# Halving a gated mixer's DFT steps by parity of 16-row blocks: small TensorE tiles for steps 1, 3 and 4, a product over all partitions, and a new hand-written order

## The chip, the core and the metric

The kernel runs on one core of one Trainium2 chip. The metric is device time in microseconds (us); the median of three runs before the change is 245.09 us (244.05 to 245.45). Five engines work side by side: TensorE (PE, with its weight loads PEld), VectorE (DVE), ScalarE (ACT), GpSimd (POOL) and SyncE (SP), which here issues all DMAs. Matmuls read SBUF (the on-chip memory of 128 partitions) and write PSUM, from which DVE or ACT must copy results out.

## The reference, cut to what matters

Two branches work on a sequence of S = 2048 rows of D = 640 channels, and a gate mixes them.

```python
x = A_q
g = sigmoid((x * gate_w).sum(-1, keepdims=True))
# branch A: a long convolution per channel, by FFT of length 2S
k_shift = sum of 4 shifted copies of k, each times shift_k[:, j]
kv = k_shift * v
y  = irfft(rfft(kv, 2S) * rfft(ssm_k, 2S))[:S] + kv * ssm_D
a  = q * y
# branch B: an MLP with shifts of the hidden rows
h  = gelu(layernorm(x) @ w1);  hs = (4 groups of h shifted by +1, -1, +2, -2 rows) @ w2
x1 = x + hs;  b = x1 + gelu(layernorm(x1) @ w3) @ w4
out = g * a + (1 - g) * b
```

All inputs and the output are bf16.

## The kernel before, in words

**Rows.** Row s = 16 t + t1 lies in partition t (0 to 127) at place t1 (0 to 15) of the free dimension, so a tile of 128 partitions x 16 x 640 holds the sequence (`q_rows`, L62 to L65).

**Branch A, the convolution.** It is a DFT of length 4096 in two stages, a product, and the inverse in two stages.

- *Taps* (`tap`, L518): the four-tap shift as matmuls with diagonal weights; they use half the rows of the array each (64 x 128 tiles), one half per 64 channels. `k` comes in by `k_load` (L497), which transposes on PE (`transposed`, L553; "A": ACT copies out) or by DMA ("D").
- *Step 1* (`step1`, L357): the DFT over t. The weights F1 (L223) have one column set per parity of t; each set has zeros in the rows of the other parity, so every matmul uses the full 128 x 128 array (L369, 512 columns; L372, 256). It runs for kv ("KV") and for the filter ("HT0"), eight blocks c of two t1 each, five units a block. Each unit takes one PSUM bank and one copy to `stg` by ACT (L320) or DVE (L322); the block is sent to DRAM (S_x or S_h).
- The filter reaches step 1 through `h_transpose` (L332): 80 PE transposes of 128 x 128, copied out by ACT (L346).
- *Gather* (L387) reads S_x or S_h back with t1 among the partitions.
- *Step 2* (`step2`, L395): the twiddled DFT over t1, on tiles of 64 rows x 32 columns, eight side by side (L413). Real parts land in partitions 0 to 63, imaginary parts in 64 to 127.
- *Product* (L430): the complex product of filter and kv, five DVE instructions for each of eight s (L434 to L442); four of them work on 64 partitions x 2560 elements, since real and imaginary parts lie in different partitions.
- *Step 3* (L445): the first inverse stage, full 128 x 128 matmuls (L456) with the weights I, built by `table` (L304) from CMP; five units of 512 columns for each s, one PSUM bank each, copied to `gs` and sent to S_g.
- `gin` (L472) loads S_g; *step 4* (L803) is the last inverse stage: two accumulating full matmuls of 320 columns (L817; F4, L239, has zeros for the other parity), then scale, gate and multiply by q (L821 and L824 on ACT and DVE, or L827 on DVE), and a total into X (L831).

**Branch B.** `x_stats`, `x_norm`, `x_turn` (layer norm and transposes), `mlp1` (L641, matmul L651, gelu L654), `h_shift` (L695, copies on DVE; `turn`, L684, shifts across the row blocks), `w2` (L723: matmul L728, add L730, sum of squares L733), `x1_norm` (L735), `w3` (L770: L776, gelu L781), `w4` (L789: L794, add L796), `scale_x1` (L783), `store` (L786).

**PSUM.** Pool "psc" (L76) has four banks and serves taps, steps 1 to 4 and the transposes; pool "psm" (L77) has two tiles of two banks for mlp1, w2, w3 and w4. The SBUF ring "row" has four slots (L69) and serves kn, xn, stg, gs, q2 and the last part of gin.

**Order.** The string ORDER (L835) lists every piece of every step by hand, with the engine of each copy ("A" or "V") in the step's name; every engine gets its instructions in this order. SP's queue carries every DMA in the same order, so a DMA that waits for its data holds up all that stand behind it.

Of the kernel before, what the change touches and what calls it, by code (L numbers as in the profile page):

```python
# [16 lines left out]
P = 128  # L17
S = 2048
D = 640
# [22 lines left out]
def kernel(  # L42
# [19 lines left out]
    q_rows = A_q.rearrange("b (p t1) d -> (b p) t1 d", t1=NT)  # L62
    o_rows = out.rearrange("b (p t1) d -> (b p) t1 d", t1=NT)
    v_rows = A_v.rearrange("b (p t1) d -> (b p) t1 d", t1=NT)
    k_rows = A_k.rearrange("b (p t1) d -> (b p) (t1 d)", t1=NT)  # L65
# [19 lines left out]
    F1 = const.tile([P, 2, P], BF16, name="F1")  # L85
    F4 = const.tile([P, 2, H, 2], BF16, name="F4")
    CMP = const.tile([P, 2, NG, 2, 32], BF16, name="CMP")
# [55 lines left out]

    def load_h(dc):
        if "E" not in st:
            st["E"] = main.tile([P, DC * F], BF16, name="E", tag="W3")
        if dc < 3:
            st["HN", dc] = st["E"][:, dc * S:dc * S + S]
        else:
            hn = ring.tile([P, S], BF16, name="HN", tag="gt", bufs=GTB)  # L150
            st["HN", dc] = hn[:]
        SP.dma_start(out=st["HN", dc], in_=A_ssm_k[dc * P:(dc + 1) * P, :])

    def load_x(c):
        SP.dma_start(out=X[:, 4 * c:4 * c + 4, :], in_=q_rows[:, 4 * c:4 * c + 4, :])

    def load_x0(h):
        SP.dma_start(out=X[:, 2 * h:2 * h + 2, :], in_=q_rows[:, 2 * h:2 * h + 2, :])
# [64 lines left out]
    def f1_table():  # L223


        ts(col(24), bit(0), -1.0, 1.0)
        stt(col(29), bit(0), -1.0, pf[:])
        ts(pf2[:], col(29), 0.5)
        n = tab([P, H, 2], "n")
        ts(n[:, :, 0], R64[:, 0:H], col(29), pf2[:])  # L230
        ts(n[:, :, 1], n[:, :, 0], float(128 + 128), op0=ALU.add)
        ts(n[:, :, 0], n[:, :, 0], float(64 + 128), op0=ALU.add)
        f = ring.tile([P, P], BF16, name="f", tag="gt", bufs=GTB)
        yield from sin_table(f[:].rearrange("p (a b) -> p a b", b=2), n, 256)
        yield
        for r in range(2):
            ts(F1[:, r, :], f[:], bit(0) if r else col(24))

    def f4_table():  # L239
# [3 lines left out]
        stt(col(1), bit(2), 4.0, col(0))  # L243
        stt(col(1), col(1), -1.0, pf[:])
        ts(col(1), col(1), 0.25, 1.0)
        stt(col(1), bit(3), 2.0, col(1))
        stt(col(1), bit(4), -2.0, col(1))
        stt(col(1), col(0), 32.0, col(1))
# [3 lines left out]
        V.memset(F4[:], 0.0)  # L252
        yield from sin_table(F4[:, 0, :, 0], n, 256)
        A.activation(out=F4[:, 1, :, 1], in_=n[:], func=ACT.Sin, scale=TWO_PI / 256 * SH, bias=NPI[:])

    def t2_table():

        ts(col(8), bit(6), -1.0, 1.0)
# [8 lines left out]
        for c in range(2):  # L267
# [6 lines left out]
            yield from sin_table(CMP[:, 0, :, c, :], n, 8192)  # L274
            yield

    def i_tables():

        ts(col(12), bit(5), -1.0, 1.0)
        ts(col(18), bit(5), 4.0, 1.0)  # L280
        stt(col(18), LOW5, 256.0, col(18))
        for c in range(2):
            ts(col(20 + c), bit(6), 2048.0, 2048.0 * (1 - c) + 4096.0)
        ag = ring.tile([P, NG], F32, name="ag", tag="gt", bufs=GTB)
        ts(ag[:], R64[:, 0:NG], 4.0, col(18))
        odd = ag[:].rearrange("p (i j) -> p i j", j=2)[:, :, 1]
        ts(odd, odd, -2.0, op0=ALU.add)
        yield
        m = ring.tile([P, NG, 32], I32, name="m", tag="gt", bufs=GTB)
        V.tensor_tensor(out=m[:], in0=ag[:].unsqueeze(2).to_broadcast([P, NG, 32]),  # L290
                        in1=R64[:, 0:32].unsqueeze(1).to_broadcast([P, NG, 32]), op=ALU.mult)
        for c in range(2):
            n = tab([P, NG, 32], "n")
            ts(n[:], m[:], col(20 + c), op0=ALU.add)
            yield from sin_table(CMP[:, 1, :, c, :], n, 8192)
            yield
# [6 lines left out]

    def table(which, ev):  # L304

        st["I"] = pool("C").tile([P, NG, P], BF16, name="I")
        for o in range(2):
            o and (yield)
            scaled(ev[o], st["I"].rearrange("p g (j c k) -> p g j c k", j=2, c=2)[:, :, o], CMP[:, 1], bit(5) if o else col(12))
# [13 lines left out]

    def cuts(a, b):
# [7 lines left out]
    def h_transpose(dc):  # L332
        if "HT0" not in st:
            st["HT0"] = main.tile([P, NT * D], BF16, name="HT0", tag="RT")
        hv = st.pop(("HN", dc)).rearrange("p (t t1) -> p t1 t", t1=NT)
        dst = st["HT0"][:].rearrange("p (t d) -> p t d", t=NT)
        def make(hh):
            box = {}

            def first():  # L340
                ps = box["ps"] = psc.tile([P, 8, P], BF16, name="pst", tag="c")
                for i in range(8):
                    PE.transpose(out=ps[:, i, :], in_=hv[:, 8 * hh + i, :], identity=IDB[:])

            def second():
                A.copy(out=dst[:, 8 * hh:8 * hh + 8, dc * P:(dc + 1) * P], in_=box["ps"][:])  # L346
# [10 lines left out]
    def step1(name, c, ev):  # L357
# [3 lines left out]
        o = 2 * c * D  # L361

        def make(u):
            box = {}

            def first():
                ps = box["ps"] = psc.tile([P, 2, 256], F32, name="ps1", tag="c")
                if u < 4:
                    PE.matmul(ps[:].rearrange("p a b -> p (a b)"), lhsT=F1[:, u % 2, :], rhs=src[:, o + 512 * (u // 2):o + 512 * (u // 2) + 512], start=True, stop=True)  # L369
                else:  # L370
                    for r in range(2):
                        PE.matmul(ps[:, r, :], lhsT=F1[:, r, :], rhs=src[:, o + 1024:o + 1280], start=True, stop=True)  # L372

            def second():
                if not stg:
                    stg.append(ring.tile([P, 2, 2 * D], BF16, name="stg", tag="row", bufs=ROW))
                if u < 4:
                    evac(ev[u], stg[0][:, u % 2, 512 * (u // 2):512 * (u // 2) + 512], box["ps"][:].rearrange("p a b -> p (a b)"))
                else:
                    evac(ev[u], stg[0][:, :, 1024:1280], box["ps"][:])  # L380
            return first, second

        def send():
            SP.dma_start(out=scr[:, :, o:o + 2 * D], in_=stg[0][:])
        return banks(5, make, [send])
# [9 lines left out]
    def step2(name, b, ev):  # L395
# [5 lines left out]
        def make(u):  # L401
            ps = []

            def first():
                for j in range(2):
                    ps.append(psc.tile([P, 512], F32, name="ps2", tag="c"))
                for lo, hi in cuts(512 * u, 512 * u + 512):
                    i = lo // D
                    for o in range(2):
                        for c in range(2):  # L410
                            for j in range(2):
                                q, r = H * c + 32 * o, slice(H * j, H * j + H)
                                PE.matmul(ps[j][q:q + 32, lo - 512 * u:hi - 512 * u], lhsT=CMP[r, 0, 8 * b + 2 * i + o, c, :],  # L413
                                          rhs=ax[i // 2][r, 2 * (i % 2) + o, lo - i * D:hi - i * D], start=True, stop=True, tile_position=(H * j, q))
# [15 lines left out]
    def product(s):  # L430

        h, x = st.pop(("hs", s)), st.pop(("xs", s))
        p2 = ring.tile([P, 4, D], BF16, name="p2", tag="HM", bufs=1)
        V.tensor_tensor(out=p2[0:64], in0=x[0:64], in1=h[64:128], op=ALU.mult)  # L434
        yield
        V.tensor_tensor(out=p2[64:128], in0=x[64:128], in1=h[0:64], op=ALU.mult)  # L436
# [3 lines left out]
        V.tensor_tensor(out=h[0:64], in0=h[0:64], in1=h[64:128], op=ALU.subtract)  # L440
        yield
        V.tensor_tensor(out=h[64:128], in0=p2[0:64], in1=p2[64:128], op=ALU.add)  # L442
        st["p", s] = h

    def step3(s, ev):  # L445
        p1 = st.pop(("p", s))
        gs = []

        def make(u):
            box = {}  # L450

            def first():
                ps = box["ps"] = psc.tile([P, 512], F32, name="ps3", tag="c")
                for a, b in cuts(512 * u, 512 * u + 512):
                    i = a // D
                    PE.matmul(ps[:, a - 512 * u:b - 512 * u], lhsT=st["I"][:, 8 * (s // 2) + 2 * i + s % 2, :], rhs=p1[:, i, a - i * D:b - i * D], start=True, stop=True)  # L456

            def second():
                if not gs:
                    gs.append(ring.tile([P, 4, D], BF16, name="gs", tag="row", bufs=ROW))  # L460
                evac(ev[u], gs[0][:].rearrange("p g d -> p (g d)")[:, 512 * u:512 * u + 512], box["ps"][:])
            return first, second
# [5 lines left out]
        return banks(5, make, [send])  # L468
# [28 lines left out]
    def k_load(c, how):  # L497
# [4 lines left out]
        if how == "D":  # L502
            return [lambda: SP.dma_start_transpose(out=dst(), in_=k_rows[:, 4 * c * D:4 * c * D + 4 * D])]

        def load():
            st["kn", c] = ring.tile([P, 4 * D], BF16, name="kn", tag="row", bufs=ROW)
            SP.dma_start(out=st["kn", c][:], in_=k_rows[:, 4 * c * D:4 * c * D + 4 * D])
# [7 lines left out]
    def v_load(c):  # L515
        SP.dma_start(out=st["KV"][:, 4 * c * D:4 * c * D + 4 * D].rearrange("p (t d) -> p t d", d=D), in_=v_rows[:, 4 * c:4 * c + 4, :])

    def tap(q, ev):  # L518
# [17 lines left out]
        for e in range(2):  # L536
# [12 lines left out]
            steps += [copied, times] if ev[e] == "A" else [both]  # L549
# [3 lines left out]
    def transposed(dst, src, how):  # L553

        def make(u):
# [8 lines left out]
            def second():  # L564
                evac(how, dst()[:, a:b, :], box["ps"][:, 0:b - a, :])
# [118 lines left out]
    def turn(E, dst, src, s):  # L684

        if s > 0:
            E.memset(dst[:, :, 0:1], 0.0)
            E.tensor_copy(out=dst[:, :, 1:P], in_=src[:, :, 0:P - 1])
        else:
            E.memset(dst[:, :, P - 1:P], 0.0)  # L690
            E.tensor_copy(out=dst[:, :, 0:P - 1], in_=src[:, :, 1:P])
# [94 lines left out]
    def store(t1):  # L786
        SP.dma_start(out=o_rows[:, t1, :], in_=X1[:, t1, :])
# [10 lines left out]
    def load_q(c):  # L798
        q2 = ring.tile([P, 4, D], BF16, name="q2", tag="row", bufs=ROW)
        SP.dma_start(out=q2[:], in_=q_rows[:, 4 * c:4 * c + 4, :])  # L800
# [235 lines left out]
```

## Time and profile before

| What | Value |
|---|---|
| median of three runs | 245.09 us |
| profiled execution, span (its own time, from first to last instruction) | 240.0 us |
| first matmul starts | 6.58 us |
| last matmul ends | 235.9 us |
| step 1, 96 matmuls (L369, L372) | 16.1 + 3.5 us from start to start |
| step 2, 512 matmuls (L413) | 12.5 us from start to start |
| step 3, 64 matmuls (L456) | 10.0 us from start to start |
| step 4, 64 matmuls (L817) | 9.4 us from start to start |
| product, 40 instructions (L434 to L442) | 59.5 us busy on DVE |
| granted TensorE clock | 1.000 |

All durations in the profile are those of one execution, whose span is 5.1 us below the median of the runs. A matmul's busy time overlaps that of the next one, so PE's busy times of groups add up to more than the span; "from start to start" is the distance from the first matmul of an unbroken run of one line to the first of the next run, added over the runs. A group's row names the line, the engine, the operation, what is written and read, the shape, and the number; then the total busy time and the mean of one in ns; then how long the engine stood idle before.

### The profile page before, as it was taken

The page shows a single profiled execution, that of the slowest core. Times are in us where ns is not written, and L with a number is a line of the kernel's source. Part 1 is how long each engine was busy: PE and PEld are TensorE (multiplying, and loading weights), DVE is VectorE, ACT ScalarE, POOL GpSimd, SP SyncE. Part 2 cuts the span into 40 slices and gives each one's busy share as a digit, 9 for nine tenths or more (in the row PEclk, how much of TensorE's full clock was granted, in tenths as well). Part 3 has the DMA queues.
Part 4 walks back from the last instruction along what each step waited for, and adds up shares of the span by engine and source line. Part 5 has one row for each costly group of instructions (what it writes and reads, how often), then busy time and mean ns, then how long its engine had stood idle before and what let it go on. Part 6 is the DMA issues. An engine that isn't in the chain of part 4 may idle for free.

```text
span 240.0 us, 5176 instructions
## 1 busy us (share of the span) xinstructions
PE 224.6 (94%) x2041; PEld 122.6 (51%) x2041; DVE 209.6 (87%) x428; ACT 176.0 (73%) x300; POOL 11.1 (5%) x26
## 2 busy tenths in 40 slices
PE   0989999999999999999999999999999999999993
PEld 0975556444865555434444444455434456456551
DVE  7999999877889999769999999999999996247895
ACT  4999999779899999999949866837568642336430
POOL 1022012000000020004200000000000000000000
PEclk9999999999999999999999999999999999999999
DMA  7999999885879959995999836976410376489933
GB/s 248 392 373 221 371 324 268 203 288 202 242 224 379 405 199 225 317 335 171 294 271 248 247 130 232 200 264 223 145 54 0 128 231 219 137 297 279 304 110 109
DMA packets 48390, 57.05 MB, mean 238 GB/s; under 512 B 23017, under 2 KB 40170, under 8 KB 48110
## 3 DMA queue, kind: packets, MB, share of 16 engines
q1 hardware_dynamic: 48366, 56.72, 76.8%
q8 instruction: 16, 0.26, 0.4%
q14 instruction: 8, 0.07, 0.1%
HBM read 33.77 MB, written 18.36 MB: 217 GB/s over the span
## 4 chain that ended last, share of the span: by engine, by line
PE 40%; DVE 32%; ACT 18%; DMA 4%; issue 4%; SPq 0%; DVEq 0%
PE ps L776 13%; PE ps L794 8%; PE psm L651 7%; ACT stg L320 4%; DVE p L436 4%; DVE p L434 4%; ACT HT L346 3%; PE ps L369 3%; DVE X L796 3%; DVE hs L442 3%; DVE hs L440 3%; DVE hs L438 3%; ACT KT L320 3%; ACT jk L733 3%; DMA q<-in_A_q_dram 2%
## 5 line engine op out<-in xcount | busy, mean ns | idle before, releaser
L794 PE MATMUL ps<-W,gt 128*128 128x512 bf16 (+1 forms) x384 | 56.9, 299 | 0.0
L776 PE MATMUL ps<-x1t,W 128*128 128x512 bf16 x240 | 55.3, 379 | 0.7 <-DVE X L796 0.7
L794 PEld LDWEIGHTS <-gt 128*128 128x128 bf16 x384 | 29.6, 98 | 24.1 <-issue 2.8
L781 ACT ACTIVATE gt<-ps 128x1024 bf16<-128x1024 f32 x24 | 24.8, 1034 | 20.5 <-PE ps L776 20.5
L776 PEld LDWEIGHTS <-W 128*128 128x128 bf16 x240 | 22.5, 98 | 27.5 <-issue 3.4
L320 ACT CAST stg<-ps 128x512 bf16<-128x512 f32 x45 | 25.1, 637 | 0.7 <-PE ps L369 0.7
L322 DVE CAST stg<-ps 128x512 bf16<-128x512 f32 x35 | 22.8, 685 | 3.1 <-PE ps L369 2.9
L320 ACT CAST gs<-ps 128x512 bf16<-128x512 f32 x33 | 17.4, 598 | 11.0 <-PE ps L456 10.0
L651 PE MATMUL psm<-xt,WA 128*128 128x512 bf16 x100 | 23.5, 379 | 0.0
L728 PE MATMUL psw<-WA,HT 128*128 128x512 bf16 (+1 forms) x116 | 21.4, 299 | 0.0
L320 ACT CAST hs<-ps 128x512 bf16<-128x512 f32 x31 | 16.5, 615 | 2.5 <-PE ps L413 2.4
L322 DVE CAST XS<-ps 128x512 bf16<-128x512 f32 x21 | 13.4, 683 | 3.4 <-PE ps L413 3.3
L821 ACT ACTIVATE y<-ps,GS 128x320 bf16<-128x320 f32 x17 | 8.1, 526 | 10.9 <-PE ps L817 7.2
L827 DVE SCALAR_TENSOR_TENSOR q<-ps,GS,q 128x320 bf16<-128x320 f32 x15 | 7.8, 545 | 9.0 <-PE ps L817 8.2
L651 PEld LDWEIGHTS <-WA 128*128 128x128 bf16 x100 | 9.6, 97 | 11.2 <-issue 0.6
L728 PEld LDWEIGHTS <-HT 128*128 128x128 bf16 x116 | 10.0, 98 | 10.0 <-issue 0.7
L796 DVE SCALAR_TENSOR_TENSOR X<-ps,OMG,X 128x640 bf16<-128x640 f32 x16 | 14.0, 878 | 0.2
L730 DVE SCALAR_TENSOR_TENSOR X<-psw,X 128x640 bf16<-128x640 f32 x16 | 12.9, 820 | 1.0 <-PE psw L728 1.0
L413 PE MATMUL ps<-ax,CMP 64*32 64x512 bf16 (+3 forms) x512 | 13.4, 300 | 0.1
L733 ACT ACTIVATE jk<-X 128x640 bf16<-128x640 bf16 x16 | 13.4, 834 | 0.0
L320 ACT CAST XS<-ps 128x512 bf16<-128x512 f32 x19 | 10.5, 606 | 3.1 <-PE ps L413 3.1
L654 ACT ACTIVATE HT<-psm 128x1024 bf16<-128x1024 f32 (+1 forms) x12 | 10.5, 885 | 3.0 <-PE psm L651 3.0
(142 smaller groups left out, 377.7 us busy)
## 6 DMA issues: line engine op xcount, KB each, us to landing
S_x<-stg SPq DMA_DIRECT2D x8, 640.0 KB, 3.8
ax<-S_x SPq DMA_DIRECT2D x8, 640.0 KB, 5.2
S_h<-stg SPq DMA_DIRECT2D x8, 640.0 KB, 8.0
ax<-S_h SPq DMA_DIRECT2D x8, 640.0 KB, 4.4
S_g<-gs SPq DMA_DIRECT2D x8, 640.0 KB, 3.2
W<-in_B_w_dram SPq DMA_DIRECT2D x2, 1920.0 KB
KV<-in_A_v_dram SPq DMA_DIRECT2D x4, 640.0 KB
q<-in_A_q_dram SPq DMA_DIRECT2D x4, 640.0 KB
```

What stands on the lines that cost most here:

```text
L320: A.copy(out=dst, in_=src)
L322: V.tensor_copy(out=dst, in_=src)
L413: PE.matmul(ps[j][q:q + 32, lo - 512 * u:hi - 512 * u], lhsT=CMP[r, 0, 8 * b + 2 * i + o, c, :], rhs=ax[i // 2][r, 2 * (i % 2) + o, lo - i ...
L651: PE.matmul(ps[:, v, :].rearrange("p (a b) -> p a b", a=4), lhsT=W1N[:, k, 160 * f:160 * f + P] if f < 4 else W1M[:, k, :], rhs=xt[:, :, k ...
L654: A.activation(out=st["HT"][:, 4 * c:4 * c + 4, 2 * u:2 * u + nf, :].rearrange("p t f b -> p f t b"), in_=ps[:].rearrange("p f (t b) -> p ...
L728: PE.matmul(ps[:, o:o + w], lhsT=h_tile(f, t1), rhs=W2P[:, f, o:o + w], start=(f == 0), stop=(f == 4))
L730: V.scalar_tensor_tensor(out=X1[:, t1, :], in0=ps[:], scalar=1.0, in1=X[:, t1, :], op0=ALU.mult, op1=ALU.add, accum_out=S12[:, 0, t1:t1 + 1])
L733: A.activation(out=jk[:], in_=X1[:, t1, :], func=ACT.Square, accum_out=S12[:, 1, t1:t1 + 1])
L776: PE.matmul(ps[:, u, :].rearrange("p (a b) -> p a b", a=4), lhsT=st["W3"][:, k, f * P:(f + 1) * P], rhs=xt[:, :, k, :], start=(k == 0), st ...
L781: A.activation(out=gt[:, 2 * (fp % 2):2 * (fp % 2) + 2, :], in_=ps[:], func=ACT.Gelu_apprx_tanh)
L794: PE.matmul(ps[:, o:o + w], lhsT=st["gt", c, f // 4][:, f % 4, i * P:(i + 1) * P], rhs=st["W4"][:, f, o:o + w], start=(f == 0), stop=(f == ...
L796: V.scalar_tensor_tensor(out=X1[:, t1, :], in0=ps[:], scalar=OMG[:, t1:t1 + 1], in1=X1[:, t1, :], op0=ALU.mult, op1=ALU.add)
```

## The change

Rows are dealt differently: with s = 32 t2 + 16 r + t1, row s now lies in partition 64 r + t2 at place t1. So the parity r of the 16-row block is the half of the partitions. The parts:

- `both` (new): every load of q, k and v is issued as two DMAs of 64 partitions; `store` also. `load_cj`, weights and scratch transfers stay as they are.
- `turn` (shifts): a shift across row blocks is now two copies, since the neighbour in partition order is in the other half.
- `h_transpose`: 160 transposes with 64 weight columns, each into half of the PSUM partitions; the copies are spread over ACT and DVE.
- `step1`: F1 has 64 rows used for each parity; for every unit two matmuls of 512 columns, one on rows 0 to 63 and one on rows 64 to 127, each into a PSUM bank of its own. Four blocks of four t1 instead of eight of two.
- `step2`: the same 512 matmuls on the same tiles, but the output is ordered so that real and imaginary parts (c) stand in separate slots of the free dimension, over all 128 partitions.
- `product`: four of its five instructions are 128 partitions x 1280.
- `step3`: the weights INV (32 rows used per tile, made directly by `i_tables`; `table` and I are gone); two units for each s, each of 16 matmuls of 320 columns on tiles of 32 rows x 64 columns, which take four PSUM banks at once and are copied out in four pieces of 320.
- `step4`: two matmuls of 320 columns, each into half of the PSUM partitions, without zeros and without accumulation.
- `tap` and `step4` get an empty step for "V", so that the numbering of steps doesn't depend on the engine.
- ORDER is new throughout, engine letters too.

```diff
+    def both(dst, rows, t, n, at):
+        for r in range(2):
+            SP.dma_start(out=dst[HALF[r], at * D:(at + n) * D], in_=rows[r][:, t * D:(t + n) * D])
...
-                    PE.transpose(out=ps[:, i, :], in_=hv[:, 8 * hh + i, :], identity=IDB[:])
+                    for r in range(2):
+                        PE.transpose(out=ps[HALF[r], i, :], in_=hv[:, 8 * hh + i, r, :], identity=IDB[:], tile_position=(0, H * r))
...
-                if u < 4:
-                    PE.matmul(ps[:].rearrange("p a b -> p (a b)"), lhsT=F1[:, u % 2, :], rhs=src[:, o + 512 * (u // 2):o + 512 * (u // 2) + 512], start=True, stop=True)
-                else:
-                    for r in range(2):
-                        PE.matmul(ps[:, r, :], lhsT=F1[:, r, :], rhs=src[:, o + 1024:o + 1280], start=True, stop=True)
+                for r in range(2):
+                    ps.append(psc.tile([P, 512], F32, name="ps1", tag="c"))
+                    PE.matmul(ps[r][:], lhsT=F1[HALF[r]].rearrange("p a b -> p (a b)"), rhs=src[HALF[r], o + 512 * u:o + 512 * u + 512], start=True, stop=True,
+                              tile_position=(H * r, 0))
...
-        V.tensor_tensor(out=p2[0:64], in0=x[0:64], in1=h[64:128], op=ALU.mult)
+        V.tensor_tensor(out=p2[:, 0, :], in0=x[:, 0, :], in1=h[:, 1, :], op=ALU.mult)
...
-        V.tensor_tensor(out=h[0:64], in0=h[0:64], in1=h[64:128], op=ALU.subtract)
+        V.tensor_tensor(out=h[:, 0, :], in0=h[:, 0, :], in1=h[:, 1, :], op=ALU.subtract)
...
-                ps = box["ps"] = psc.tile([P, 512], F32, name="ps3", tag="c")
-                for a, b in cuts(512 * u, 512 * u + 512):
-                    i = a // D
-                    PE.matmul(ps[:, a - 512 * u:b - 512 * u], lhsT=st["I"][:, 8 * (s // 2) + 2 * i + s % 2, :], rhs=p1[:, i, a - i * D:b - i * D], start=True, stop=True)
+                for i in range(4):
+                    ps.append(psc.tile([P, W], F32, name="ps3", tag="c"))
+                for c in range(2):
+                    for h in range(2):
+                        for i in range(4):
+                            a = slice(32 * i, 32 * i + 32)
+                            PE.matmul(ps[i][HALF[h]], lhsT=INV[a, 4 * (s // 2) + 2 * h + s % 2, 1 - c:3 - c, :].rearrange("p a b -> p (a b)"),
+                                      rhs=y[a, c, h, W * v:W * v + W], start=(c == 0), stop=(c == 1), tile_position=(32 * i, H * h))
...
-            E.tensor_copy(out=dst[:, :, 1:P], in_=src[:, :, 0:P - 1])
+            E.tensor_copy(out=dst[:, :, H:P], in_=src[:, :, 0:H])
+            E.tensor_copy(out=dst[:, :, 1:H], in_=src[:, :, H:P - 1])
...
-                    PE.matmul(ps[:], lhsT=F4[:, r].rearrange("p a b -> p (a b)"), rhs=g[:, r, o + 320 * v:o + 320 * v + 320], start=(r == 0), stop=(r == 1))
+                    PE.matmul(ps[HALF[r]], lhsT=F4[:], rhs=g[:, r, o + 320 * v:o + 320 * v + 320], start=True, stop=True, tile_position=(0, H * r))
```

In the new ORDER the five loads of the filter (`load_h`) stand together behind the second block of kv's step 1, where before they were spread over the first part; W4's load stands behind all of the filter's step-1 stores, where before two of these came after it; the last step of the list is now step 4's total of t1 = 12, where before it was the store behind w4's add of t1 = 15.

## Prediction

> **What bounds the kernel now.** I read the shares of each engine first, then the 40 slices, then windows of 15 us, then TensorE's own timeline.
>
> ```profile
> PE 224.6 (94%) x2041; PEld 122.6 (51%) x2041; DVE 209.6 (87%) x428; ACT 176.0 (73%) x300; POOL 11.1 (5%) x26
> ...
> PE   0989999999999999999999999999999999999993
> ...
> DVE  7999999877889999769999999999999996247895
> ACT  4999999779899999999949866837568642336430
> ```
>
> PE is full from the second slice to the last but one. VectorE is full too, up to slice 33, ScalarE mostly up to slice 22. The windows (stretch, its length, then busy us and instruction count of PE, PEld, DVE, ACT, POOL, then granted clock, DMA share, GB/s) show that PE stays full whichever of the others does. The chain of waits puts only 40% on PE because it goes through VectorE wherever both are full:
>
> ```profile
> PE 40%; DVE 32%; ACT 18%; DMA 4%; issue 4%; SPq 0%; DVEq 0%
> ```
> ```profile
> 120.00:135.00 15.00, 15.00 (x180) 6.94 (x178) 14.67 (x16) 11.85 (x20) 0.00 (x0) 1.00 1.07 271
> ...
> 195.00:210.00 15.00, 15.00 (x101) 8.10 (x99) 8.43 (x9) 3.61 (x5) 0.00 (x0) 1.00 0.62 197
> ```
>
> A busy PE can be a waiting PE, so I took distances from the start of one run of matmuls to the start of the next (first column below; the second column counts overlap).
>
> ```profile
> 46.20 2.32 PE L651 MATMUL psm<-xt,WA 128*128 128x512 bf16 x10
> 48.35 1.03 PE L369 MATMUL ps<-KV,F 128*128 128x512 bf16 x4
> 49.22 2.32 PE L651 MATMUL psm<-xt,WA 128*128 128x512 bf16 x10
> ```
> ```profile
> 97.34 2.32 PE L776 MATMUL ps<-x1t,W 128*128 128x512 bf16 x10
> 99.59 0.63 PE L413 MATMUL ps<-ax,CMP 64*32 64x512 bf16 x24
> 100.15 2.33 PE L776 MATMUL ps<-x1t,W 128*128 128x512 bf16 x10
> 102.41 0.85 PE L413 MATMUL ps<-ax,CMP 64*32 64x384 bf16 x32
> 103.19 2.33 PE L776 MATMUL ps<-x1t,W 128*128 128x512 bf16 x10
> 105.45 0.63 PE L413 MATMUL ps<-ax,CMP 64*32 64x512 bf16 x16
> ```
>
> Ten 512-column matmuls take 2.15 us between others of the full array (46.20 to 48.35): 0.2155 each. That is the price of 512 columns. Adding columns at this price over the whole kernel, with 0.117 us for each change of tile shape (worked out below), gives 216.3 us: transposes 10.6, taps 8.6, mlp1 21.6, z 1.1, step 1 17.3, w2 21.7, w3 51.7, step 2 8.6, step 3 8.6, step 4 8.6, w4 51.7, 52 changes 6.1. From the first matmul (6.58) to the end of the last (235.9) pass 229.3 us. So all waits inside PE's list are 13.0 us, 3.3 of them in the first 60 transposes (6.8 us for 3.5 of work, behind ScalarE's copies of KT). **PE's own list is the bound.** 240.0 is 6.6 of start, 216.3 of PE, 13.0 of waits and 4.1 of tail.
>
> **The price of a change of tile shape.** Step 2 is the one step in small tiles between full ones. Before it, ten w3 matmuls take 2.25 to 2.26 (97.34 to 99.59, 100.15 to 102.41) in place of 2.155: 0.10 more. Its own runs of 16 and 24 matmuls are two units of 512 columns with eight tiles side by side, 0.431 us, and take 0.56: 0.13 more. One excursion costs 0.233, one change 0.117. The taps (64 rows by 128 columns, L534) agree: 44 at 33.47 take 1.87 to 35.34, 1.72 of columns if both halves run side by side and 3.45 if not. So half-row tiles do run in pairs, and 0.14 goes to the change.
>
> **Part by part.**
>
> Step 1 (L369, L372; new L363). 64 matmuls of 512 and 32 of 256 columns, half of whose weight rows are zero, become 80 of 512 on half-row tiles: 40 pairs of 0.2155 = 8.6 in place of 17.3, **−8.7**. The taps are the row for the pairing; nothing side by side would be 0.
>
> Step 3 (L456; new L450). 64 full matmuls, 20,480 columns, 8.6 us, become 256 of 320 columns on eight tiles: 10,240 columns, 4.3 us, **−4.3**. The nearest row is step 2, 512 of 320 on average at 24 ns.
>
> Step 4 (L817; new L815). 64 of 320 columns, 8.6 us, now in pairs on half-column tiles: **−4.3**. Row: z_rows, 20 of 512 columns in 1.18 us, four side by side (4.3 one after another).
>
> The transposes of the filter (L343) go from 80 to 160 with 64 weight columns, in pairs: 5.0 again; one after another 160 × 62 ns = 10. I take 0, up to +5.
>
> Changes of shape. In the changed program's instruction order on PE I count them: 52 before, 159 after, because the step-1, step-3 and step-4 runs stand between full-array runs (25, 16 and 8 runs). 107 × 0.117 = **+12.5**. Below: 0, if they hide. Above: a single tap (19.87 to 21.09, 1.21 for 0.86) would make it 0.175 each, +18.7. I take the step-2 row, the only one with twenty repeats. PE's list: −8.7 −4.3 −4.3 +12.5 = **−4.8**, to 211.5.
>
> [...]
>
> VectorE. Product: five instructions of 1,488 ns (L434 to L442, four of them 64 partitions × 2560) become four of 128 × 1280 and one as before. Between 640 elements (L831, 483 ns) and 2560 (L438, 1,489) 1280 is 818: 8 × (7.44 − 4.76) = −21.4. Copies of step 3: 7 of 512 (687 ns) become 23 of 320, at most 545 each (L827): +7.7. Step-1 copies 35 to 25: −6.9. Seven copies of the filter's transposes come from ScalarE: +4.7 at the 676 of a 1024-wide xt copy (L322). Five x_norm (439) and three scale (382) more: +3.3; step 4: 8 fewer of 545, 8 more of 318: −1.8; tables about −4, the shifts' doubled copies +1. Two KT copies come too (+1.4), two of hs (+1.4). Together about −15. It buys nothing directly: PE was full in 120 to 135 while DVE was. ScalarE: ten copies of step 1 more (+6.4), seven HT copies fewer (−7.4), step-3 copies 33 × 598 to 41 × at most 526 (+1.9), step 4 +8 × 527 (+4.2), x_norm and scale −7.5, tables −3, but seven loads of function tables for four (3 × 1.28 = +3.9), KT and hs −3: about −4.5. Both have more slack; of the 9.7 us of waits inside the list after the first transposes I give back 2. Bounds: 0, and all 9.7.
>
> Start. Four issues of X stand before the first k in place of two (0.44 us each): kn may land 0 to 0.9 later. VectorE now takes two of nine KT copies, 1.8 us of ScalarE's 6.9. Together **−1.0** (between +0.9 and −1.8).
>
> Queue. SP issues 34 more DMAs (halves of 64 partitions): 34 × 0.45 = 15 us of its time. SP waits in line for its data nearly all the time, so this is hidden in the middle. In the tail 32 stores for 16 are about 13 us of issue in some 24. What stands behind them is load_q.3 and the last stores. The kernel now ends with a total (L829, 0.48) and two issues after w4's last add: **+0.9** (0 to 2).
>
> Moved loads. W4 was issued at 96.6, landed at 104.9 and was first read at 114.5; from the last step-1 run to the first w4 PE's list had 17.2 us and now has 14.0, so 9.6 of cover become about 6. The five loads of the filter (512 KB each), spread over 8.9 to 44 us before, now stand together some 10 us of PE's list ahead of their transposes; 2.5 MB at the 250 GB/s of slices 8 to 10 are 10 us. I take 0 for both; +3 if the filter is late, which the upper end below contains.
>
> **Sum.** 240.0 − 4.8 − 2.0 − 1.0 + 0.9 = 233.1 of span. The runs' median, 245.09, is 5.1 above the profiled span; with it **238.2 us**.
>
> **Rivals.**
> (a) Forecast: changes cost what step 2 shows, PE stays full: 235 to 242.5. Chance 0.44.
> (b) Changes cost less where only rows or only columns are cut, or the waits go as well: half of the 12.5 is −6, all of the waits −7.7 more: 225 to 234, middle 232. For it: DVE and ACT have slack. Against: the taps, rows only, pay 0.14 + 0.10. Chance 0.18.
> (c) PSUM slots become the bound, slower than before. The pool "psc" has four banks. Before, step 3 took one at a time (L453), now four at once; step 1 takes two. A step-3 run can't start until four copies are out, and the next unit of any step waits for its four. 14 of 16 runs have at least one copy on VectorE, behind a product instruction (1.49 or 0.82) or w4's add (0.88). It decides when the copies come out later than the w3 or w4 run between (1.6 to 2.2 us). At one short product instruction each, 14 × 0.8 = 11: 249. At one long one and an add, 14 × 2.4 = 33. Against: before, PE waited for step-3 copies only once, 0.3 us. Chance 0.25.
> (d) The tiles don't run side by side, the change doesn't do what it says: +17.3 and +5: 260. The taps and z speak against. Chance 0.05.
> (e) Halved DMAs eat it: the first 15 us and the tail are paced by SP, +6: 244. Chance 0.08.
>
> **Numbers.** Likeliest (a): 238.2, its own range 235 to 242.5. To leave out no more than 2 in 10 I go from 231 (within b) to 249 (within c). 0.5% is 1.2 us, about what a measurement of this kernel can tell. Faster by more: a and b, 0.62. Within: e, 0.08. Slower: c and d, 0.30.
>
> **What would show it.** Step-1 runs of four matmuls: 0.43 + 0.23 = 0.66 from start to start (0.86 if unpaired, 0.43 if changes are free). Step-3 runs of 16: 0.27 + 0.23 = 0.50. w3 runs of ten beside them 2.26. Product instructions of 1280 at 0.82. PE's span from first matmul to last about 222. Wrong if PE has waits over 0.5 us ahead of L450 or L363 released by gs or stg copies (c), or if step-3 runs take over 0.6 without a wait.

## The result and the profile after

The changed kernel takes 258.04 us (median; 257.56 to 258.53), the kernel before 244.57 in the same comparison: a ratio of 1.058, with a 95% interval of 1.052 to 1.065. The forecast was 238.2, range 231 to 249. The profiled execution of the kernel after has a span of 256.2 us.

Page of the kernel after: busy us of each engine, then the slices (PEclk is the granted TensorE clock), then the chain of waits by engine.

```profile
PE 223.2 (87%) x2278; PEld 114.3 (45%) x2297; DVE 193.4 (76%) x454; ACT 172.5 (67%) x310; POOL 13.0 (5%) x26
...
PE   0387789999899998999999999999999999579960
...
DVE  7757499889766878987789895888987974057970
ACT  0979399779966898899679776764674544145630
...
PEclk9999999999999999999999999999999999959995
...
PE 66%; DMA 17%; DVE 5%; ACT 5%; SPq 3%; issue 2%; DVEq 0%; ACTq 0%
```

VectorE lost 16.2 us of work and ScalarE 3.5, as forecast (15 and 4.5). PE was to stay full; it isn't in the first six slices, in the 35th and 36th and at the end. DMA rose from 4% to 17% of the chain, DVE fell from 32% to 5%.

To place the difference I cut the span at four events, read from PE's timeline: the first matmul, the filter's first transpose, the end of the last step-1 run, the start of w3's last 40 matmuls.

| Stretch, us | before | after | difference |
|---|---|---|---|
| start to first matmul | 6.58 | 9.60 | +3.0 |
| to the filter's first transpose | 54.3 | 59.2 | +4.8 |
| to the end of step 1 | 36.44 | 40.70 | +4.3 |
| to w3's last 40 matmuls | 106.86 | 102.93 | −3.9 |
| to the end of the last matmul | 31.67 | 34.99 | +3.3 |
| tail | 4.11 | 8.79 | +4.7 |

Of the rows that were to get shorter only the fourth did, and more than half of that is work that moved. One w3 run of ten matmuls stands ahead of the last step-1 run in the kernel after; before, all of w3 stood behind it (the timeline at 97.34 in the prediction).

```profile
106.65 2.33 PE L773 MATMUL ps<-x1t,W 128*128 128x512 bf16 x10
108.92 0.60 PE L363 MATMUL ps<-HT,F 64*128 64x512 bf16 x4
```

Its 2.27 us belong to the third row in one kernel and to the fourth in the other. With the same work in each row they would read +2.0 and −1.7. (The profiled execution of the kernel before was a quick one. The two kernels of the last experiments that start with the same DMAs have their first matmul at 8.15 and 8.16, so some 1.6 of the first +3.0 is spread. A span lies 1.8 below its own execution's time in the kernels run since, so a typical span of the kernel before is about 242.)

The end first. Windows of the kernel after (columns as in the prediction: PE, PEld, DVE, ACT, POOL, granted clock, DMA share, GB/s), and then its PE timeline:

```profile
221.20:225.60 4.40, 0.00 (x0) 0.00 (x0) 0.00 (x0) 0.00 (x0) 0.00 (x0) 0.73 0.97 307
225.60:230.00 4.40, 4.03 (x19) 2.01 (x21) 3.30 (x9) 2.81 (x5) 0.00 (x0) 0.50 1.02 405
```
```profile
213.69 7.50 PE L773 MATMUL ps<-x1t,W 128*128 128x512 bf16 x34
225.64 2.13 PE L815 MATMUL ps<-gin,F 128*64 128x320 bf16 x14 [4.45 <-DMA gin<-S_g]
228.11 3.52 PE L792 MATMUL ps<-W,gt 128*128 128x512 bf16 x11 [0.33 <-issue]
231.56 0.73 PE L815 MATMUL ps<-gin,F 128*64 128x320 bf16 x8
```

All engines stand still for 4.4 us while the DMAs are full: step 4 waits for gin. Behind it the granted clock is 0.50, and w4's first run takes 3.45 from start to start in place of 2.69. In the tail SP's timeline shows the last 24 half stores back to back:

```profile
237.48 16.17 SPq L785 DMA_DIRECT2D out_dram<-X  x24
```

That is 0.67 us each, to 253.65, while the last matmul ended at 247.4.

Now the start. One window each, from 7 to 15 us, of the kernel before and of the kernel after:

```profile
7.00:15.00 8.00, 7.26 (x88) 6.77 (x88) 7.67 (x21) 7.75 (x12) 1.22 (x2) 1.00 1.03 397
```
```profile
7.00:15.00 8.00, 4.61 (x40) 4.11 (x40) 5.32 (x13) 6.88 (x12) 2.85 (x2) 1.00 1.05 213
```

The last two columns decide. The DMA engines are as busy (1.03, 1.05), but they move 213 GB/s in place of 397. Busy DMA engines aren't fast ones here: the packets got slower (those of 5,120 bytes from a mean of 205 ns to about 370 in the first 15 us).

**Theory:** a DMA over 64 neighbouring partitions moves its bytes at half the rate, and that costs most of the loss; the rest is the unpaired transposes and the place of load_q in SP's queue. **Rivals:** the doubled distance of the rows in DRAM; SP's issues; a loss inside PE's list (the changes of tile shape, PSUM slots).

### The profile page after: what moved, and what is told of

Same layout as the page of the kernel before. It is cut to its first block, busy times and chain, and to the rows that moved or that the text cites. A ratio compares the mean times of both kernels' runs of the same rounds, so it can differ in the third digit from the quotient of the medians.

```text
span 256.2 us, 5750 instructions
## 1 busy us (share of the span) xinstructions
PE 223.2 (87%) x2278; PEld 114.3 (45%) x2297; DVE 193.4 (76%) x454; ACT 172.5 (67%) x310; POOL 13.0 (5%) x26
## 4 chain that ended last, share of the span: by engine, by line
PE 66%; DMA 17%; DVE 5%; ACT 5%; SPq 3%; issue 2%; DVEq 0%; ACTq 0%
PE ps L792 21%; PE ps L773 18%; PE psw L725 6%; DMA KV<-in_A_v_dram 5%; PE ps L403 5%; PE pst L337 4%; DMA X<-in_A_q_dram 4%; DMA S_h<-stg 3%; PE psm L646 3%; PE ps L363 3%; PE ps L450 3%; PE ps L815 3%; DMA S_g<-gs 2%; DMA gin<-S_g 2%; SPq L150 2%
## 5 line engine op out<-in xcount | busy, mean ns | idle before, releaser
L792 PE MATMUL ps<-W,gt 128*128 128x128 bf16 (+1 forms) x371 | 56.6, 300 | 1.4 <-issue 1.0
L310 ACT CAST stg<-ps 128x512 bf16<-128x512 f32 x55 | 29.7, 592 | 5.4 <-PE ps L363 4.7
L310 ACT CAST gs<-ps 128x320 bf16<-128x320 f32 x41 | 15.1, 433 | 15.5 <-PE ps L450 12.1
L725 PE MATMUL psw<-WA,HT 128*128 128x128 bf16 (+1 forms) x110 | 20.9, 296 | 1.3 <-DVE X L727 0.9
L819 ACT ACTIVATE y<-ps,GS 128x320 bf16<-128x320 f32 x25 | 11.8, 528 | 13.9 <-PE ps L815 13.2
L312 DVE CAST stg<-ps 128x512 bf16<-128x512 f32 x25 | 16.6, 683 | 3.0 <-PE ps L363 2.3
L312 DVE CAST gs<-ps 128x320 bf16<-128x320 f32 x23 | 10.5, 485 | 8.8 <-PE ps L450 7.7
L557 PE MATMUL pst<-IDB,kn 128*128 128x128 bf16 x60 | 7.0, 311 | 11.0 <-DMA kn<-in_A_k_dram 10.3
L725 PEld LDWEIGHTS <-HT 128*128 128x128 bf16 x116 | 9.3, 98 | 11.6 <-issue 4.1
L825 DVE SCALAR_TENSOR_TENSOR q<-ps,GS,q 128x320 bf16<-128x320 f32 x7 | 3.7, 548 | 13.4 <-PE ps L815 13.4
L529 PE MATMUL psk<-DG,KT 64*128 64x256 bf16 (+3 forms) x190 | 11.3, 244 | 2.5 <-ACT yk L537 1.7
```

Source lines behind the costliest of these rows:

```text
L310: A.copy(out=dst, in_=src)
L312: V.tensor_copy(out=dst, in_=src)
L529: PE.matmul(ps[e][:, lo:hi, :], lhsT=kt[a], rhs=st["DG"][a, 4 * k + lo - i:4 * k + hi - i, a], start=(i == 0), stop=(i == 7))
L725: PE.matmul(ps[:, o:o + w], lhsT=h_tile(f, t1), rhs=W2P[:, f, o:o + w], start=(f == 0), stop=(f == 4))
L792: PE.matmul(ps[:, o:o + w], lhsT=st["gt", c, f // 4][:, f % 4, i * P:(i + 1) * P], rhs=st["W4"][:, f, o:o + w], start=(f == 0), stop=(f == ...
L819: A.activation(out=box["y"][:], in_=box["ps"][:], func=ACT.Copy, scale=GS[:, t1:t1 + 1])
```

## The experiments

Each ratio is against the kernel before, run on the same chip, with its 95% interval. That kernel's own median lies between 242.56 and 244.57 us in these comparisons, so a difference in us between runs of two comparisons can be off by up to 2 us.

**1. The half DMAs alone, on the kernel before.**

```diff
+    def two(dst, src):
+        for r in range(2):
+            SP.dma_start(out=dst[HALF[r]], in_=src[HALF[r]])
-        SP.dma_start(out=X[:, 4 * c:4 * c + 4, :], in_=q_rows[:, 4 * c:4 * c + 4, :])
+        two(X[:, 4 * c:4 * c + 4, :], q_rows[:, 4 * c:4 * c + 4, :])
```

> The kernel before, with one thing of the change: each load of X, k, v and q and each store goes as two DMAs of 64 partitions (0 to 63, 64 to 127); rows, DRAM strides, order and arithmetic stay. Theory (a DMA that touches 64 partitions moves its bytes at about half the rate of one over 128): packets of 5,120 bytes in the first 15 us rise from 205 to about 370 ns, the first matmul comes 1 to 3 us later (6.6 to about 8.5), the filter's first transpose 3 to 5 us later, the tail grows by 3 to 4 us; 250 to 256 us. Rival 1 (the doubled distance between DRAM rows slows the packets, not the number of partitions): packets stay at 205 ns, and only the 34 more issues cost, mostly in the tail: 246 to 249. Rival 2 (nothing of this matters, the loss is in TensorE's list): 244 to 246.

Measured: 259.33 us, 1.064 (1.061 to 1.068), more than the whole change costs, and more than the theory's 250 to 256. Rows, tiles and order are the old ones. The window from 7 to 15 us:

```profile
7.00:15.00 8.00, 4.58 (x40) 4.11 (x40) 4.06 (x6) 4.79 (x7) 0.00 (x0) 1.00 1.05 213
```

213 GB/s again, without any change of the DRAM distance. The filter's first transpose comes 14.4 us later; from there to w3's last matmuls nothing changes (+36.42 and +106.84); the end and the tail take 3.7 more. The half DMAs are enough for the loss. PE also ran part of the start at a lower granted clock here (0.70 from 20 to 30 us, 0.89 from 45 to 60, where the kernel after has 1.00 in both), so not all of the 14.4 us is transfer time.

**2. One DMA over all partitions, with the halves on the DRAM side.**

```diff
-        for r in range(2):
-            SP.dma_start(out=dst[HALF[r], at * D:(at + n) * D], in_=rows[r][:, t * D:(t + n) * D])
+        SP.dma_start(out=dst[:, at * D:(at + n) * D], in_=whole(rows, t, n))
+    # whole: DRAM pattern [[16 * D, 2], [32 * D, 64], [1, n * D]]
```

> The kernel after, with each pair of half DMAs (X, k, v, q, stores) put into one DMA over all 128 partitions whose DRAM side walks the same doubled row distance; the two DMA transposes stay halved. Theory (64 partitions are slow): packets of the first 15 us fall back from 370 to about 205 ns, the first matmul from 9.6 to about 7, the stage up to the filter's first transpose from 68.8 to about 63, the tail from 8.8 to about 4.5, and the last wait of PE (4.45) shrinks: 244 to 249 us. Rival 1 (DRAM distance): packets stay at 370, only the tail's issues are saved: 253 to 256. Rival 2 (no part): 257 to 259.

Measured: 431.0 us. Neither theory foresaw this, and as a test of the DRAM distance it is void. The window from 7 to 15 us:

```profile
7.00:15.00 8.00, 0.00 (x0) 0.00 (x0) 2.05 (x6) 0.00 (x0) 0.00 (x0) 1.00 0.17 52
```

52 GB/s at a DMA share of 0.17, about an eighth of 397 at about a sixth of the DMA share. From 20 to 50 us its queue's packets take 12.7% of the time of 16 engines, as much as two of them have. Why so little isn't shown: the slowest dimension of the DRAM pattern is 2 here, and no run changes that alone.

**3. load_q.2 behind gin.0.2 in the order.**

```diff
- ... w3.3.3:1 load_q.2:0 w3.3.2:0 w3.3.4:1 gin.0.2:0 w3.3.5:0 ...
+ ... w3.3.3:1 w3.3.2:0 w3.3.4:1 gin.0.2:0 load_q.2:0 w3.3.5:0 ...
```

> The kernel after, with one item of the order moved: load_q.2 behind gin.0.2, whose data PE waits for 4.45 us at the end of w3. Theory (load_q's 640 KB share the DMA engines with gin): gin lands 1.5 to 3 us sooner, the idle stretch falls to 2 or 3 us, and if the half clock that follows it for 6.8 us (step 4's first 14 matmuls 2.5 us, w4's twelve 3.45 in place of 2.69) goes with it, 2 us more: 253 to 256. Rival (gin is issued only when the last S_g send has landed at 219.7, and that send is what is late): gin lands within 0.7 us of before, 257 to 258.5.

Measured: 256.07 us, 1.050 (1.046 to 1.054), 2.0 less than the kernel after. PE's wait shrank from 4.45 to 3.60, and the half clock behind it from 6.8 to 3.4 us; but w4's first run still met it. gin is issued at 218.2 in place of 219.7, as soon as the last S_g has landed. So load_q was a part of it. The rest is the way of the last S_g through DRAM: in the kernel after its send, issued at 213.46, lands 6.23 us later, and gin behind it takes 5.89. The kernel before has the same 40 w3 matmuls in this place and no wait. Its last send goes out at 204.48, and gin is issued at 207.74, 3.5 us after these matmuls begin, against 7.3 in the kernel after and 6.5 here. Why the sends land later isn't shown.

**4. Whole transposes of the filter.**

```diff
-                    for r in range(2):
-                        PE.transpose(out=ps[HALF[r], i, :], in_=hv[:, 8 * hh + i, r, :], identity=IDB[:], tile_position=(0, H * r))
+                    PE.transpose(out=ps[:, i, :], in_=hv[:, 8 * hh + i], identity=IDB[:])
```

> The kernel after, with the filter's 160 transposes of 64 weight columns replaced by the 80 of 128 columns of the kernel before; the rows of the filter then stand in the old order, so its part of the result is computed on permuted rows. Theory (half-column transposes do not run side by side): the L337 group falls from 9.6 to 5.4 us and the end by 4: 253 to 255. Rival (their time hides a wait for the filter or for the copies, which then shows in its place): 256.5 to 258.5.

Measured: 251.61 us, 1.034 (1.028 to 1.040), 6.4 less than the kernel after; 4 was expected. One run of the half-width transposes in the kernel after, and one of the whole ones here:

```profile
76.30 3.78 PE L337 MATMUL pst<-IDB,E 128*64 128x128 bf16 x64
```
```profile
73.67 2.35 PE L336 MATMUL pst<-IDB,E 128*128 128x128 bf16 x32 [0.28 <-DVE HT L312]
```

The start of the next run is at 80.24 and 76.07, so a half-width transpose takes about 60 ns and a whole one 75 here (62 in the kernel before): the halves don't run side by side. Filter to end of step 1 fell by 3.6, as the theory said. A further 2.6 came at the end, where the wait for gin fell to 1.31 and no half clock followed: the last send of S_g takes 4.83 us in place of 6.23, and gin 4.16 in place of 5.89. Why isn't shown.

**5. The old rows and whole DMAs, all else as after.**

```diff
-        rows = a.rearrange("b (t2 r t1) d -> (b t2) r (t1 d)", r=2, t1=NT)
-        return [rows[:, r, :] for r in range(2)]
+        return a.rearrange("b (p t1) d -> (b p) (t1 d)", t1=NT)
```

> The kernel after with the DMAs of the kernel before: X, k, v and q are loaded and the result is stored in the old row order by one DMA over 128 partitions each, the DMA transposes of k too; nothing else is undone, so the small tiles of steps 1, 3 and 4 compute on permuted rows. Theory (the loss outside TensorE's list is the half DMAs'): filter's first transpose back from 68.8 to 61 or 62, tail from 8.8 to about 5, the stages between as in the kernel after (+40.7 and +102.9): span 241 to 244, time 243 to 247, about the kernel before. Rival (the new order or the waits for copies cost what was lost): 250 or more.

Measured: 245.19 us, 1.008 (1.005 to 1.012): 12.9 us less than the kernel after. The window from 7 to 15 us:

```profile
7.00:15.00 8.00, 5.90 (x64) 5.20 (x65) 6.57 (x15) 6.37 (x10) 3.72 (x2) 1.00 1.02 402
```

402 GB/s, the filter's first transpose at 61.1, the tail 4.30; the stretches between are those of the kernel after (+40.86 and +102.93). The theory held on both sides now: adding the halves costs 15.4, taking them away gives 12.9 (12.0 when each run is set against its own kernel before).

**6. The same, with whole transposes and the moved load_q.2** (both edits above).

> The run before this one, with the 80 whole transposes of the filter in place of 160 of half width (filter rows in the old order, its part computed on permuted rows), and load_q.2 behind gin.0.2. Theory (what is left is the forecast's sum): a further 3.6 to 4.2 us for the transposes and 1.5 to 2 for the order: 237 to 241, that is 3 to 7 below the kernel before. Rival (those savings only showed because DMAs were late): 243 to 246.

Measured: 238.29 us, 0.979 (0.973 to 0.985). The theory's range holds. This run is the nearest to what the forecast's sum describes; how its parts compare is said below. As it works on permuted rows, it computes another result and isn't a version to use.

**7 and 8. The second halves from another queue,** ScalarE's or GpSimd's, in the complete kernel.

```diff
-            SP.dma_start(out=dst[HALF[r], ...
+            (SP, A)[r].dma_start(out=dst[HALF[r], ...
```

> The kernel after, complete, with the second half (partitions 64 to 127) of each load of X, k, v, q and of each store issued by ScalarE in place of SyncE, so that both halves can be under way on the DMA engines at once. Theory (half a DMA is slow because its 64 partitions share half the way into the core's memory, not because of the packet): packets of the first 15 us fall from 370 to 250 or less, the filter's first transpose comes 4 to 7 us earlier: 248 to 254, less what ScalarE loses by about 20 issues and their waits (0 to 6). Rival (a packet to 64 partitions takes 370 ns whatever runs beside it): 256 to 262.

> As the run before this one, with GpSimd issuing the second halves, which has nothing else to do after the first tables. Theory: the same gain at the start, and the tail shorter than in the run on ScalarE, since no copy of step 4 waits behind a store: 246 to 252; the price of an issue on GpSimd is not known from any row so far: at 1 us each it is hidden except in the first 10 us (some +2). Rival: 256 to 262.

Measured: 261.2 us, 1.072 (1.066 to 1.078), and 255.81, 1.047 (1.041 to 1.054): the first is within the rival's range, the second just below it and 3.8 above the theory's. The window from 7 to 15 us, with ScalarE and then with GpSimd:

```profile
7.00:15.00 8.00, 3.52 (x32) 3.27 (x33) 5.17 (x12) 4.40 (x8) 1.22 (x2) 1.00 1.03 206
```
```profile
7.00:15.00 8.00, 4.30 (x39) 4.04 (x40) 5.81 (x15) 6.16 (x10) 3.90 (x3) 1.00 1.02 268
```

With ScalarE it is 206 GB/s: there the halves under way together are no faster, and the rival was right. With GpSimd it is 268, with packets of 5,120 bytes at some 300 ns in this window, where the kernel after has some 380: there they are faster, though not as fast as whole ones (397). So a packet to 64 partitions isn't slow whatever runs beside it. The start gained nothing from this: the first matmul comes at 10.69 and the filter's first transpose at 69.14, against 9.60 and 68.76 in the kernel after, and PE waits 4.7 us for W1's load in place of 1.9. Why the two queues differ isn't shown. The 1 us for an issue on GpSimd in the expectation was my guess, from no row. On ScalarE the stretch between w3 and the last matmul is also 4.8 us longer (39.77 for 34.99), which I put down to the issues without a test; what GpSimd gained, 2.2, is mostly the tail (6.14 for 8.79).

**9. Even and odd partitions in place of lower and upper,** on the kernel before.

```diff
-    HALF = (slice(0, H), slice(H, P))
+    HALF = (slice(0, P, 2), slice(1, P, 2))
```

> The kernel before with the same DMAs in two as in the first experiment, but by even and odd partitions in place of lower and upper 64: as many DMAs, bytes and packets, the DRAM distance doubled as in the kernel after, and all 128 partitions' neighbourhoods touched by each DMA. Theory (what halves the rate is that the 16 DMA engines share the way into 64 neighbouring partitions): 5,120-byte packets of the first 15 us at about 205 ns in place of 370, some 400 GB/s from 7 us on, the filter's first transpose at 61 to 64 in place of 75.3; what is left is the issues: 245 to 249. Rival (a DMA with 64 rows is slow wherever they lie, as each engine has half as many packets in flight, or because of the DRAM distance): packets at 370 and 256 to 261.

Measured: 247.73 us, 1.018 (1.014 to 1.022), 11.6 less than with lower and upper halves. The window:

```profile
7.00:15.00 8.00, 5.65 (x60) 5.12 (x60) 5.27 (x13) 6.12 (x10) 0.63 (x1) 1.00 0.97 335
```

335 GB/s (387 from 10 to 15 us; the theory had some 400 from 7 us on), and the filter's first transpose at 63.2, with the same number of DMAs, bytes and rows, and with the DRAM distance doubled. So neither the number of partitions nor the distance is the cause, but which partitions a DMA touches. The shared way into the memory that this theory and run 7's name stands in no trace; what is measured are the rates from 7 to 15 us: 213 with lower and upper halves, 335 with even and odd, 397 whole, and with two queues 206 (run 7) and 268 (run 8). What is left over the kernel before, 3.9 us, I put down to the issues; the part that can be seen is the tail, 6.5 in place of 4.1.

**10. A complete kernel with the old rows:** as run 6, but steps 1 and 4 as full matmuls, half of whose weights are zero.

```diff
-                    PE.matmul(ps[r][:], lhsT=F1[HALF[r]]..., rhs=src[HALF[r], ...], tile_position=(H * r, 0))
+                    PE.matmul(ps[r][:], lhsT=F1[:, r, :], rhs=src[:, o + 512 * u:o + 512 * u + 512], start=True, stop=True)
```

> A complete kernel that keeps the gains which showed and drops the price: row order and DMAs of the kernel before, 80 whole transposes of the filter, steps 1 and 4 as full matmuls with half of the weights zero (80 of 512 and 64 of 320 columns), and from the kernel after step 3 on small tiles, the product on all partitions, the order (with load_q.2 behind gin.0.2). Theory: the run with old rows, whole transposes and the moved load (238.3), plus step 1 back to 17.3 from 12.3 and step 4 from 7.0 to 8.7 or 9.4, less the changes of tile shape beside these runs (25 and 8 runs, 0.107 each in the neighbour: 3.5): 240 to 243, that is 0.3 to 1.5% below the kernel before. Rival (full matmuls hold VectorE's and ScalarE's copies up, the order was made for the short runs): 244 to 248.

Measured: 243.55 us, 0.999 (0.997 to 1.001): no difference from the kernel before, 0.55 above the theory's range.

**11. The product and step 3 alone, in the old order.**

```diff
-    def step3(s, ev): ...  five units, one bank each
+    def step3(s, ev): ...  two units, four banks each (as after; its steps put into the old places)
```

> The kernel before with only one part of the change: step 2 writes both parts of a frequency to the same partition, the product works on all partitions, step 3 runs on eight small tiles (with its tables and the row order of step 4's table); rows, DMAs, transposes, steps 1 and 4 and the order stay, except that the ten steps of step 3 are fitted into the old places. Theory (the stretch from the last step-1 run to the last w3 block fell by 4.0 us in every run with this part, whatever the DMAs did): 2.7 us less in step 3 and the rest from VectorE's waits, 236 of span, 239 to 241.5. Rival 1 (that stretch got shorter only by the new order): step 3's 2.7 less the waits for four banks at once, 242 to 245. Rival 2 (four banks taken at once hold the neighbours up in an order not made for them): 245 to 249.

Measured: 248.39 us, 1.024 (1.019 to 1.030): slower. The theory falls, rival 2 holds. More than half of the 4.0 us that the theory counted on was the w3 run that stands elsewhere in the new order. From the last step-1 run to w3's last 40 matmuls this run takes 113.09, 6.2 more than the kernel before with the same work there, and step 3 takes 13.4 us from start to start, in place of 7.3. PE's timeline:

```profile
142.11 2.33 PE L773 MATMUL ps<-x1t,W 128*128 128x512 bf16 x10
144.37 0.32 PE L452 MATMUL ps<-hs,INV 32*64 32x320 bf16 x2
145.87 0.80 PE L452 MATMUL ps<-hs,INV 32*64 32x320 bf16 x14 [1.18 <-ACT gs L312]
146.60 2.33 PE L773 MATMUL ps<-x1t,W 128*128 128x512 bf16 x10
```

The run of 16 at 144.37 starts while the last one's copies are under way, gets two matmuls out and then waits 1.18 us for a bank.

**12. The old order up to the end of step 1, the new one behind it** (complete, old rows).

```diff
- ORDER of before, with its last part
+ ORDER of before up to the last step-1 run, then that of after, less what is done by then
```

> A complete kernel: the order of the kernel before up to its last step-1 run, with its rows, DMAs, transposes, step 1 and functions; from there the order of the kernel after (load_q.2 behind gin.0.2) with its product on all partitions and step 3 on small tiles, step 4 in full matmuls. Theory (the old order costs nothing up to there, and the new one is worth 4 us behind it because it leaves room for four banks at once): 97.3 to the last step-1 run, then 134.6 as in the hybrid of the run before last and up to 3 for one w3 run and two step-2 units that the new order had done by then, tail 4.3: 236 to 239.5 of span, 240 to 242.5, at most 1.5% below the kernel before. Rival (the joint itself costs waits): 243 to 247.

Measured: 243.95 us, 1.002 (0.999 to 1.005): as the kernel before, within the rival's range. Behind the joint all of w3 stands as in the kernel before, and the two stretches there take 106.13 and 32.63, for 106.86 and 31.67: in this setting the new order with the small tiles of step 3 is worth nothing. No complete kernel here beats the one before.

## Why the prediction was wrong

**The step that failed** is "Queue", and the start's −1.0 with it. I counted the 34 more DMAs by SP's issues (15 us, hidden) and so put the transfers themselves at nothing, without asking what a DMA over 64 partitions does to the bytes. The runs show 213 GB/s in place of 397 from 7 to 15 us, and the first matmul 3.0 us later (some 1.6 of it spread) in place of 1.0 earlier. The halves cost 12.9 us when taken out of the kernel after and 15.4 when put into the one before. Rival (e) named the right edit and the right places, the first 15 us and the tail, but its price was SP's time, +6 to 244, at a chance of 0.08. Its mechanism is only part of the loss: even and odd halves, with as many issues, cost 3.9.

**The filter's transposes**, taken at 0 with up to +5: +3.6 to +4.2. The upper price, 160 × 62 = 10, is what they took (9.6). The row I leaned on, tiles side by side, was one of matmuls with other row or column tiles of 512 columns; no row showed transposes paired.

**Moved loads**, taken at 0: W4 was no trouble. But I looked only at the moved loads I had listed. load_q.2 ahead of gin.0.2, and last S_g sends that landed late, cost 4.45 of PE plus the half clock; moving load_q gave 2.0 (1.4 when each run is set against its own kernel before).

**The tail**, +0.9 (0 to 2): +4.7. 0.67 us for each half store, back to back. Whole stores (run 5) give 4.30, so the total behind w4's last add costs next to nothing.

**What held.** A run of four step-1 matmuls takes 0.54 from start to start and costs its neighbour 0.11, 0.65 together (0.66 forecast); a step-3 run of 16 takes 0.41 and 0.11 beside it (0.50), the w3 runs beside are 2.26, product instructions of 1280 elements 0.82. So the changes of tile shape cost what step 2 had shown.

**The sum,** by contrast, was partly lucky where it came near. Run 6 has neither the half DMAs nor the half-width transposes nor load_q in the way, and is 5.4 below the kernel before, forecast 6.9. But from its first matmul to its last PE takes 225.9 us for 229.3, 3.4 less, where the forecast had 6.8 less (4.8 of PE's list, 2.0 of waits; "about 222"). With the moved w3 run counted where it stood before, 0.4 of the 3.4 came up to the end of step 1, where the prediction's prices give 2.9 (8.7 less 25 excursions of 0.233), 1.7 from there to w3's last 40 matmuls, and 1.3 behind. A part of what is missing in the first stretch is PE's clock, 0.88 from 7 to 15 us in that run. The profiled spans differ by 3.6 (236.4 and 240.0); the other 1.8 lie between that execution of the kernel before and its median.

**Rival (c), PSUM slots,** didn't decide the kernel after: no wait of PE over 0.32 us there stands ahead of step 1 and none ahead of step 3, though two of its 16 runs took 0.64 and 0.91 us in place of 0.41. It isn't a phantom. Run 11 shows it at work, +6.2 where the kernel after has −1.7 for the same work: by these two, the new order is what makes room for four banks at once.

**The account.** 243.7 before; −5.4 for the small tiles, product and order on old rows (run 6: 238.3); +6.9 for the half-width transposes and load_q's place (run 5: 245.2); +12.9 for the half DMAs: 258.0. Why GpSimd's queue moved the halves faster than ScalarE's, and why the last S_g lands sooner in run 4, stays open.

## What to carry to other kernels

When a layout moves rows to the other half of the partitions, price its loads and stores before its matmuls: look at GB/s beside the DMA share, for at nearly the same share (1.05 and 1.03) the rate here was 213 in place of 397. Here the small tiles, with the product and the order, were worth 5.4 us (run 6), and what feeds them (half DMAs, half-width transposes) cost 19.8 on top, most of it at the start and in the tail, where nothing covers it. When two orders are compared by stretches, count the work in each: a moved w3 run made 1.7 us look like 3.9. And an order written by hand belongs to the instruction shapes it was made for: the same step 3 came with −1.7 us in one order and +6.2 in another.

## What the runs showed of the hardware that I had not expected

- Which 64 partitions matters, not that there are 64: 0 to 63 then 64 to 127 at 213 GB/s, even then odd at 335, all 128 at 397 (7 to 15 us). The halves issued from SP and GpSimd together reached 268, from SP and ScalarE 206.
- A DMA whose DRAM side has a slowest dimension of 2 ran at 52 GB/s, with a DMA share of 0.17.
- After an idle stretch of 4.45 us PE got half its clock for 6.8 us, after 3.60 for 3.4 us, after 1.31 and 1.41 not at all, each ahead of step 4. The half clock begins within the idle stretch (in the kernel after the granted clock is 0.73 over 4.40 us of it), so part of it falls on no work. A longer idle stretch didn't always bring more of it: 2.33 us in run 4 had no half clock behind it, 1.97 in run 7 had 3.4 us of it, 2.18 in run 1 6.8.
